# First batch of a sliding-window attention and mixer kernel: last 64 tokens as a group of their own, scores in halves, two pairs loaded raw

## The chip, the cores and the metric

The kernel runs on one core of one Trainium2 chip. Its engines are TensorE (PE; its weight loads are shown as PEld), VectorE (DVE), ScalarE (ACT), GpSimd (POOL) and SyncE (SP), each with an instruction stream of its own that runs in order; SP, ScalarE and POOL also issue DMA transfers. The metric is the time of one execution on the device in microseconds (us). Each kernel is run several times, and the median counts.

## The reference

Eight batches of causal attention over a window of 128 tokens with a linear bias per head, and a mixer over tokens and channels behind it:

```python
scores = q @ k.T / sqrt(64) - slope[h] * |i - j|        # 8 batches, 8 heads, 576 tokens, 64 wide
mask   = (i - j >= 0) & (i - j < 128)
x      = softmax(where(mask, scores, -1e9)) @ v         # heads side by side: (8, 576, 512)
u      = x + (relu(x.T @ w_tok1) @ w_tok2).T            # over tokens: 576 -> 256 -> 576
out    = u + relu(u @ w_ch1) @ w_ch2                    # over channels: 512 -> 1536 -> 512
```

Inputs and output are float32 in memory; matmuls run on bf16.

## The kernel before

Tokens are cut into blocks of 128: four blocks and a tail of 64 per batch. Scores are held transposed (keys on partitions), so that the exponential's result is at once the left operand of the product with v; v carries a column of ones, whose product is the softmax's sum. A block needs the keys of its own block and of the one before ("kind" 1 and 0). Each exponential is multiplied on VectorE with a table `masks` (or `maskt` for tails) that holds exp(-slope x distance) and zeros; for two head pairs of the first batch the bias is instead added by TensorE into the score's bank before the exponential (`BIAS`, matmuls of `slant` by `dist`, line 948).

Nothing is scheduled by hand. Every step is a `plan.op` with an engine, a cost in ns, a rank and the buffers that it makes, uses or reads; `Plan.run` plays the program through once while it is built, with the written costs and a model of the load queue, always starting the step that can begin first and then the one of least rank. The order in which steps were started becomes the order of each engine's instructions. Where the plan sees TensorE wait over 250 ns within the first 60 us, it puts in matmuls of zeros (line 1513). Constants such as `WIDE`, `START` or `WARM` are numbers of that plan; they give no instruction.

PSUM has eight banks of 512 columns. Scores take pairs of banks: `TWO` is (0,1) and (2,3). Single results take one of `ONE`, banks 4 to 7; some take `ANY`.

The program has these parts: `opening` (batch 0's attention and token mixing, head pair by head pair), then for every batch b `main` (hidden layer `uT` by `WC1`, line 1280, and output layer by `WC2` and its sums `WT`, line 1457) together with `side` (attention and token mixing of batch b+1, scores line 711, values line 769, mixing lines 814 to 892).

In `opening` a head pair hp goes through
- `turn`: 8 transposes each of q and k (line 926), copied out of PSUM to `qkT` (line 929),
- `score`: into all four banks 0 to 3, two per head of the pair: the bias (line 948), 14 score matmuls of the four blocks and four of the tail (line 968), two exponentials of 1024 columns (line 975), for pairs 2 and 3 the multiplication (line 985). The tail's scores stand in the place that block 0 would have for a block before it; so the first score needs the tail's q and k,
- `value`: products with v for each head (line 1011), reciprocal and norm (lines 1019, 1022), then the tail's own (lines 1046 to 1053),
- `mix`: both token matmuls, the residual, and the transposes for the hidden layer (lines 1066 to 1118). The first hidden-layer matmuls are those at line 1266.

Pair hp's `value` and `mix` are created right after `score` of pair hp+1.

At the start SP and ScalarE load q and k of pair 0 and of the tail as float32 (`raws`, lines 485 and 487), and VectorE casts them (lines 560, 563). All other loads are issued by POOL in the order of `LOADS`, cast to bf16 on the way, at most eight under way: q and k of pairs 1 to 3 (line 544), v (line 537), the blocks of batch 1 (line 528; q4 to q7, tails last) and the weights (line 549; W: token layers, A: quarters of `WC1`, B: quarters of `WC2`). A load into a buffer that is still read waits on POOL, and all later ones behind it. From batch 2 on q and k are transposed by DMAs on SP's queue (line 663), among the stores of the output.

Of the kernel before, what the change touches and what calls it, by code (L numbers as in the profile page):

```python
# [20 lines left out]
class Buf:  # L21
    def __init__(self, ring, choice):
        self.ring, self.choice, self.slot = ring, choice, None
        self.writers, self.parts, self.users, self.later = [], {}, [], []

# [5 lines left out]
class Ring:  # L31
# [23 lines left out]
    def take(self, b):  # L55
        b.slot = self.best(b.choice)[1]
        for i in b.slot:
            self.owner[i] = b
            self.log[i].append(b)
# [6 lines left out]
class Plan:  # L66
# [60 lines left out]
    def run(self):  # L127
# [25 lines left out]
        free = {"PE": 1500.0, "ACT": 5600.0, "DVE": 3300.0, "POOL": 1250.0, "SP": 1300.0}  # L153
# [57 lines left out]
        while todo:  # L211
            best = None
            for e, c in cand.items():
                pick, early = None, None
                for o in c:
# [9 lines left out]
                    for b in o.bufs:  # L225
                        if b.slot is None:
                            got = b.ring.best(b.choice, asked.count(b.choice))
                            asked.append(b.choice)
# [77 lines left out]
    def emit(self, spin):  # L306
# [12 lines left out]
        for _, _, go in sorted(work, key=lambda w: w[:2]):  # L319
# [6 lines left out]
PIECES = 3  # L326
HOLD = 2
# [4 lines left out]
WIDE = 1000  # L332
# [16 lines left out]
SECOND_LATE = False  # L349
BANKS = 8  # L350
# [3 lines left out]
START = 2400.0  # L354
# [14 lines left out]
FIRST_BLOCK = (2, 3)  # L369
# [3 lines left out]
def kernel(  # L373
# [48 lines left out]
    ANY = ONE + [(0,), (1,), (2,), (3,)]  # L422

# [20 lines left out]
    raws = [const.tile([P, DM], F32, name=f"raw{i}") for i in range(3)]  # L444
    plan.ring("ob", raws + [sb.tile([P, DM], F32, name=f"ob{i}") for i in range(3)])
# [38 lines left out]
    for raw, t, eng in ((raws[0], q, nc.sync), (raws[1], k, nc.scalar)):  # L484
        eng.dma_start(out=raw.rearrange("p (h n) -> p h n", h=2), in_=wide_rows(t, 0))
    for i, (t, eng) in enumerate(((q, nc.sync), (k, nc.scalar))):
        eng.dma_start(out=raws[2][i * R : (i + 1) * R, :].rearrange("p (h d) -> p h d", h=H), in_=rows(t, 0, NC * P, R))
# [16 lines left out]
    for e in range(2):  # L504
        for i, h in enumerate(HEADS[e]):
            act_.activation(out=masks[:, e, i, :, :], in_=dist[:, 0:2, :], func=ACT.Exp, scale=-float(slopes[h]))
# [50 lines left out]
    for i_, name in enumerate("qk"):  # L557
        raw = raws[i_]
        buf = block(0, 0)["qk"]
        block(0, 0)[name] = plan.op("DVE", 455, lambda raw=raw, buf=buf, i="qk".index(name): dve_.tensor_copy(  # L560
            out=buf()[:, i, :, :], in_=raw.rearrange("p (h d) -> p h d", h=H)), -1e6, makes=buf, after=4.4e3 + 600 * i_)
    for i in range(2):
        plan.op("DVE", 455, lambda i=i, buf=last["qk"]: dve_.tensor_copy(
            out=buf()[0:R, i, :, :], in_=raws[2][i * R : (i + 1) * R, :].rearrange("p (h d) -> p h d", h=H)), -1e6 + 1,
            makes=last["qk"], after=5.4e3 + 500 * i)
    lo_ = {}
    for h in [h for h in range(2, H) if h // 2 in BIAS + FIRST_BLOCK]:
# [6 lines left out]
    lw1, lw2, lw2t, lc1, lc2, later = [], [], [], [], [], []  # L574
    for item in LOADS.split():
# [7 lines left out]
        elif what == "W":  # L583
            if n == 1:
                lw1 += weights([(W1[:, 0:NC, :], w1, 512, 2080)] +
                               [(W1p[i * R : (i + 1) * R, i, :], moe_w_tok1[NC * P : S, :], 64, 420) for i in range(2)])
            else:
                lw2 += weights([(W2[:, :, :], w2[:, :, 0 : NC * P], 256, 2630)])
        elif what == "T":
            lw2t += weights([(W2t[:, :, :], w2[:, :, NC * P : S], 256, 300)])  # L590
        elif what == "A":
            hs = slice(n * DCH // 4, (n + 1) * DCH // 4)
            lc1 += weights([(WC1[:, :, hs], c1[:, :, hs], 512, 2500)]) * (NHT // 4)
# [43 lines left out]
    for e in range(2):  # L637
# [5 lines left out]
        mt.append(plan.op("DVE", 1300, go, 0, after=30e3))  # L643
# [47 lines left out]
    def scores(pr, blk, half, rank, behind=()):  # L691
# [32 lines left out]
        for e in range(2):  # L724
# [9 lines left out]
            def mask(es=es):  # L734
# [4 lines left out]
                         needs=mt if tail and half != 0 else [])  # L739
# [58 lines left out]
    def token_mix(b, rank):  # L798
# [20 lines left out]
        def tails():  # L819
            for j in range(NJ):  # L820
# [8 lines left out]
                uses=[xt] if xt else [], needs=lw1, mode=0 if pad else 1)  # L829
# [76 lines left out]
    def opening(rank):  # L906
# [7 lines left out]
        def turn(hp):  # L914
# [632 lines left out]
```

## Time and profile before

| | us |
|---|---|
| median of 3 runs | 283.03 |
| lowest and highest run | 281.44, 283.85 |
| the profiled execution: span | 281.4 |
| its TensorE busy | 271.3 |
| its VectorE busy | 209.9 |
| its ScalarE busy | 136.1 |
| its POOL busy | 115.7 |

The profiled execution's time is its span, from the first instruction to the last; it stands at the lower end of the runs. Times of single rows are counted from the span's start. A timeline row reads: start, length, engine, line, operation, output <- inputs, shape, how many; in brackets how long the engine had been idle before it and what it then waited for. A row on a load ends with the time from its issue to its landing. TensorE is busy nearly throughout, so a saving on another engine counts only where TensorE waits for it.

### The profile page before, as it was taken

How to read it: one execution, taken by the hardware profiler on the slowest of the kernel's cores; microseconds unless marked ns; L12 is line 12 of the kernel's file. 1: busy time of each engine (PE TensorE's matmuls, PEld its weight loads, DVE VectorE, ACT ScalarE, POOL GpSimd, SP SyncE). 2: the span in 40 equal slices, each digit the busy share in tenths (PEclk: the TensorE clock that was granted, in tenths of full speed). 3: DMA queues.
4: the chain of work that ended last, by engine and by line, in shares of the span. 5: the costliest groups of instructions: out<-in, count | busy, mean ns of one | idle time of the engine just before them, and what ended most of it. 6: DMA issues, size and time to landing. Idle time of an engine off the chain costs nothing.

```text
span 281.4 us, 7149 instructions
## 1 busy us (share of the span) xinstructions
PE 271.3 (96%) x2890; PEld 183.2 (65%) x2890; DVE 209.9 (75%) x493; ACT 136.1 (48%) x215; POOL 115.7 (41%) x148
## 2 busy tenths in 40 slices
PE   5799999999999999999999999999999999999994
PEld 3577556577577745486657745486657755489983
DVE  6359778998798749683979459683979469697972
ACT  6365778132983268305962069206962078205500
POOL 8998596840089105900386006900480320012000
PEclk9799999999999999999999999999999999999999
DMA  8999999999999996999799997999799830042014
GB/s 157 161 132 178 180 155 186 154 145 170 186 73 127 176 227 57 142 144 181 169 123 151 187 223 51 143 150 196 140 128 117 203 98 2 19 112 115 2 51 137
DMA packets 160337, 38.32 MB, mean 136 GB/s; under 512 B 146544, under 2 KB 159472, under 8 KB 160304
## 3 DMA queue, kind: packets, MB, share of 16 engines
q0 software_dynamic: 110512, 19.90, 90.0%
q1 hardware_dynamic: 48992, 17.57, 34.1%
q8 instruction: 22, 0.36, 0.6%
q10 hardware_dynamic: 800, 0.39, 0.5%
q14 instruction: 11, 0.09, 0.1%
HBM read 35.85 MB, written 9.44 MB: 161 GB/s over the span
## 4 chain that ended last, share of the span: by engine, by line
PE 87%; DVE 6%; DMA 3%; ACT 2%; issue 1%; SPq 0%; DVEq 0%; ACTq 0%
PE ps L1457 25%; PE ps L1280 24%; PE ps L769 5%; PE ps L711 5%; PE ps L857 4%; PE ps L1323 4%; PE ps L814 4%; PE ps L1368 4%; PE ps L1204 3%; DMA raw<-in_q_dram 3%; DVE WT L612 1%; PE ps L1266 1%; PE ps L968 1%; PE ps L892 1%; PE ps L853 1%; PE ps L1011 1%
## 5 line engine op out<-in xcount | busy, mean ns | idle before, releaser
L1286 ACT ACTIVATE r<-ps 128x512 bf16<-128x512 f32 x74 | 43.6, 602 | 78.9 <-PE ps L1280 73.0
L1280 PE MATMUL ps<-uT,WC 128*128 128x512 bf16 x324 | 79.4, 379 | 0.0
L528 POOL DMA_DIRECT2D v<-in_v_dram x36 | 30.5, 849 | 90.9 <-PE ps L769 87.6
L726 ACT ACTIVATE pe<-ps 128x1024 bf16<-128x1024 f32 (+1 forms) x64 | 55.3, 916 | 3.0 <-PE ps L711 2.3
L1280 PEld LDWEIGHTS <-WC 128*128 128x128 bf16 x324 | 28.5, 98 | 28.5 <-issue 0.7
L1457 PEld LDWEIGHTS <-r 128*128 128x128 bf16 x384 | 37.0, 98 | 8.5 <-issue 1.8
L736 DVE TENSOR_TENSOR pe<-pe,mask 128x1024 bf16<-128x1024 bf16 (+1 forms) x56 | 34.1, 619 | 10.2 <-ACT pe L726 9.7
L528 POOL DMA_DIRECT2D qk<-in_q_dram x35 | 30.4, 871 | 4.7 <-DMA WC<-in_moe_w_ch_dram 2.4
L528 POOL DMA_DIRECT2D qk<-in_k_dram x35 | 30.4, 872 | 3.7 <-DMA WC<-in_moe_w_ch_dram 1.9
L1457 PEld LDWEIGHTS <-s 128*128 128x128 bf16 x288 | 28.1, 98 | 4.7 <-DVE s L1305 0.2
L1457 PE MATMUL ps<-WC,r 128*128 128x256 bf16 x192 | 25.4, 273 | 0.0
L785 DVE TENSOR_TENSOR xb<-ps,rt 128x256 bf16<-128x256 f32 (+1 forms) x61 | 24.8, 418 | 0.6
L1457 PE MATMUL ps<-WT,s 128*128 128x256 bf16 x192 | 23.7, 273 | 0.1
L1457 PE MATMUL ps<-WT,r 128*128 128x256 bf16 x192 | 23.7, 273 | 0.0
L769 PEld LDWEIGHTS <-pe 128*128 128x128 bf16 (+1 forms) x480 | 18.3, 99 | 7.7 <-DVE pe L736 2.1
L769 PE MATMUL ps<-v,pe 128*128 128x65 bf16 (+1 forms) x480 | 22.1, 194 | 0.1
L875 DVE TENSOR_TENSOR ub<-ps,xb 128x512 bf16<-128x512 f32 x32 | 19.8, 682 | 2.0 <-PE ps L857 2.0
L711 PEld LDWEIGHTS <-qkT 64*128 64x128 bf16 x480 | 12.9, 94 | 9.3 <-issue 7.2
L1440 POOL DMA_DIRECT2D out_dram<-ob x5 | 3.6, 718 | 35.6 <-DVE ob L1428 35.4
L782 DVE RECIPROCAL rt<-ps 128x4 f32<-128x4 f32 (+1 forms) x64 | 10.4, 176 | 8.8 <-PE ps L769 8.5
L711 PE MATMUL ps<-qkT 64*128 64x128 bf16 (+1 forms) x256 | 16.8, 218 | 0.0
L1428 DVE TENSOR_TENSOR raw<-ps,ub 128x512 f32<-128x512 f32 x16 | 10.7, 686 | 6.3 <-PE ps L1457 6.3
(131 smaller groups left out, 396.9 us busy)
## 6 DMA issues: line engine op xcount, KB each, us to landing
qk<-in_q_dram POOLq DMA_DIRECT2D x31, 128.0 KB, 5.8
qk<-in_k_dram POOLq DMA_DIRECT2D x31, 128.0 KB, 6.0
v<-in_v_dram POOLq DMA_DIRECT2D x28, 128.0 KB, 6.2
out_dram<-raw SPq DMA_DIRECT2D x13, 256.0 KB, 4.3
WC<-in_moe_w_ch_dram POOLq DMA_DIRECT2D x8, 384.0 KB, 8.2
out_dram<-ob SPq DMA_DIRECT2D x11, 256.0 KB, 2.7
out_dram<-ob POOLq DMA_DIRECT2D x5, 256.0 KB, 2.9
v<-in_v_dram POOLq DMA_DIRECT2D x16, 64.0 KB, 3.9
```

The lines of the kernel that those rows point to most:

```text
L528: nc.gpsimd.dma_start(out=to()[p0 : p0 + n, :, :], in_=rows(src, b, s0, n))
L711: pe_.matmul(wide(e)[:, i, kind, a:z], lhsT=ts[kb]()[e * D : (e + 1) * D, NHP + i, :], rhs=ts[blk]()[e * D : (e + 1) * D, i, a:z], start=T ...
L726: act_.activation(out=pb()[:, e, :, lo:, c0:c1_], in_=wide(e)[:, :, lo:, c0:c1_], func=ACT.Exp, scale=scale)
L736: dve_.tensor_tensor(out=o, in0=o, in1=heads(mk, es), op=ALU.mult)
L769: pe_.matmul(view()[a:z, at, i, :], lhsT=pb()[:, e, i, kind, a:z], rhs=vb()[:, h, 0 : D + 1], start=m == 0, stop=m == len(mms) - 1, skip_g ...
L785: dve_.tensor_tensor(out=x4(), in0=view()[r0:r1_, :, :, 0:D], in1=rt()[r0:r1_, 0:n, :, :].broadcast_to([r1_ - r0, n, 4, D]), op=ALU.mult)
L814: pe_.matmul(t1[j]()[:, :], lhsT=W1[:, c, j * P : (j + 1) * P], rhs=xb()[:, blk, :], start=c == 0, stop=False)
L857: pe_.matmul(ht()[:, hs], lhsT=W2[:, j, c * P : (c + 1) * P], rhs=r1()[:, j, :], start=j == 0, stop=j == NJ - 1 and not fold)
L875: plan.op("DVE", 690, lambda blk=blk, ht=ht, hs=hs: dve_.tensor_tensor(out=ub()[:, blk, :], in0=ht()[:, hs], in1=xb()[:, blk, :], op=ALU.a ...
L1280: pe_.matmul(ct()[:, :], lhsT=WC1[:, cb, t * P : (t + 1) * P], rhs=uT()[:, cb, :], start=cb == 0, stop=cb == NCB - 1)
L1286: plan.op("ACT", 600, lambda t=t, ct=ct: act_.activation(out=r2()[:, t, :], in_=ct()[:, :], func=ACT.Relu), rk, part=(r2, t), uses=[ct], o ...
L1457: pe_.matmul(bk()[:, c * HN : (c + 1) * HN], lhsT=l(t, c), rhs=w(t), start=first, stop=g == 1 and t == HK - 1, skip_group_check=True)
```

## The change

In `opening`:
- The tail leaves `score` and `value` and becomes `ends`: one bank pair with the scores of all eight heads' 64 last tokens, one exponential, one multiplication, one set of value products, one reciprocal and one norm. It is created after pair 2's `value`.
- `score` makes two halves of two blocks. A half holds both heads in one pair of banks, taken from (0,1), (2,3) and (4,5). The first half's exponential has 768 columns, since block 0 has no block before it; the second's has 1024. Pairs 2 and 3 are multiplied in three steps: 512, 256 and 1024 columns. Their bias matmuls for block 0 go.
- q and k of pair 1 too are loaded raw by SP and ScalarE, ahead of the tail's, and cast on VectorE or ScalarE.
- Ranks are written out: scores and transposes by pair, values 1.5 pairs later, `ends` after 2.5, all of `mix` after 3 or more.
- `masks` is made by steps that the plan orders.

`LOADS` begins with v0, q2, k2; W1 comes after q3 and k3; `WC1`'s quarters come in the order 0, 2, 1, 3; one of the two copies of the last token rows (`W1p`) moves behind batch 1's blocks. A buffer may have a gate: `second`'s and `unit`'s banks are then taken from banks 4 to 7 alone until the next batch's last score has been started in the plan. Costs and due times of the plan change.

```diff
+    def options(self):
+        if self.gate and self.gate[0] is not None and self.gate[0].t0 is None:
+            return self.gate[1]
+        return self.choice
...
-LOADS = ("q1 k1 v0 v8 q2 k2 v1 W1 q3 k3 v2 v3 W2 q4 k4 v4 A0 q5 k5 v5 "
-         "A1 A2 A3 q6 k6 v6 q7 k7 v7 T0 lq8 lk8 lv8 B0 B1 B2 B3")
+LOADS = ("v0 q2 k2 v1 q3 k3 v8 W1 v2 v3 W2 A0 q4 k4 A2 v4 A1 q5 k5 v5 A3 "
+         "q6 k6 v6 q7 k7 v7 P0 T0 lq8 lk8 lv8 B0 B1 B2 B3")
...
-FIRST_BLOCK = (2, 3)
...
+    SPS = TWO + TWICE[:MORE]
...
-    raws = [const.tile([P, DM], F32, name=f"raw{i}") for i in range(3)]
-    plan.ring("ob", raws + [sb.tile([P, DM], F32, name=f"ob{i}") for i in range(3)])
+    raws = [const.tile([P, DM], F32, name=f"raw{i}") for i in range(2 * RAW + 1)]
+    plan.ring("ob", raws + [sb.tile([P, DM], F32, name=f"ob{i}") for i in range(5 - 2 * RAW)])
...
-    for raw, t, eng in ((raws[0], q, nc.sync), (raws[1], k, nc.scalar)):
-        eng.dma_start(out=raw.rearrange("p (h n) -> p h n", h=2), in_=wide_rows(t, 0))
+    for hp in range(RAW):
+        for raw, t, eng in ((raws[2 * hp], q, nc.sync), (raws[2 * hp + 1], k, nc.scalar)):
+            eng.dma_start(out=raw.rearrange("p (h n) -> p h n", h=2), in_=wide_rows(t, hp))
...
-                               [(W1p[i * R : (i + 1) * R, i, :], moe_w_tok1[NC * P : S, :], 64, 420) for i in range(2)])
+                               [(W1p[0:R, 0, :], moe_w_tok1[NC * P : S, :], 64, 250)])
...
+        elif what == "P":
+            lw1p += weights([(W1p[R:P, 1, :], moe_w_tok1[NC * P : S, :], 64, 250)])
...
         def score(hp):
-            sp = [bank(TWO) for _ in range(2)]
...
+            for part in range(2):
+                sp = bank(SPS)
+                blks = [2 * part, 2 * part + 1]
...
+                def go(blks=blks, wide=wide):
+                    f = t().rearrange("p a b -> p (a b)")
+                    for i, blk in enumerate(blks):
+                        own = slice(blk * P, (blk + 1) * P)
+                        for kind in (1, 0) if blk else (1,):
+                            kb = blk - 1 + kind
+                            for e in range(2):
+                                es = slice(e * D, (e + 1) * D)
+                                pe_.matmul(wide(e)[:, i, kind, :], lhsT=f[es, KO + kb * P : KO + (kb + 1) * P], rhs=f[es, own],
+                                           stop=True, start=hp not in BIAS, skip_group_check=True)
...
+                x = plan.op("ACT", 172 + 2 * (DM - a) / 1.2, expo, rk, uses=[sp], part=(pb, ("x", part)),
+                            **({} if part else {"makes": pb}))
...
+        def ends():
+            rk = -1e6 + ENDS_AT
+            tt = qkT[0, TAIL]
+            sp, pb = bank(SPS), plan.buf("pe")
...
+            plan.op("PE", 260, go, rk, makes=sp, uses=[tt] + ts, reads=[(x, 1) for x in ts], mode=1)
...
+            plan.op("ACT", 1026, lambda: act_.activation(out=flat(), in_=sp()[:, :], func=ACT.Exp, scale=scale), rk,
+                    makes=pb, uses=[sp])
+            plan.op("DVE", 700, lambda: dve_.tensor_tensor(
+                out=p4(), in0=p4(), in1=masks[:, :, :, :, 0:R].rearrange("p e i k c -> p (e i) k c"), op=ALU.mult), rk,
+                adds=pb, needs=mk_ops[0] + mk_ops[1])
...
+            plan.op("PE", 480, value, rk, makes=ots, uses=[pb, vt] + [held[0, hp]["v"] for hp in range(NHP)], mode=2)
...
         for hp in range(NHP):
             turn(hp)
             score(hp)
             if hp:
                 value(hp - 1)
-                mix(hp - 1)
+        ends()
         value(NHP - 1)
-        mix(NHP - 1)
+        for hp in range(NHP):
+            mix(hp)
```

More of the change, by code (lines that the diff above doesn't have):

```diff
@@ L738, in scores @@
             op = plan.op("DVE", 154 + len(es) * n / 1.92, mask, rank, part=(pb, e), reads=[(pb, ("x", i)) for i in es],
-                         needs=mt if tail and half != 0 else [])
+                         needs=mk_ops[e] + (mt if tail and half != 0 else []))
             if one:
@@ L972, in score @@
[L972 to L978 removed]
+            done = []
@@ L998, in value, with rest @@
+                def rest():
+                    o = pb()[:, :, 0, 1, :]
+                    dve_.tensor_tensor(out=o, in0=o, in1=masks[:, :, hp, 1, :], op=ALU.mult)
+                done[-1] = plan.op("DVE", 154 + (1 + part) * 267, most, rk, needs=mk_ops[0] + mk_ops[1] + [x], part=(pb, ("m", part)))
+                if not part:
+                    done.append(plan.op("DVE", 287, rest, rk, needs=mk_ops[0] + mk_ops[1] + [x], part=(pb, "r")))
+            pb.parts[0] = pb.parts[1] = done
         def value(hp):
+            rk = -1e6 + VALUE_AT + hp * STEP
@@ L1508 @@
                 o.behind.append(marks["score"])
+            for x in gates:
+                x[0] = marks["score"]
         base += n
```

202 lines of the change are left out of this document (106 added, 96 removed).

## The prediction

> **What bounds the kernel now.** I read the page first, then the busy times by stage, the timeline of the first 60 us engine by engine, the landings of single loads, and last the instruction orders of both programs.
>
> ```profile
> span 281.4 us, 7149 instructions
> PE 271.3 (96%) x2890; PEld 183.2 (65%) x2890; DVE 209.9 (75%) x493; ACT 136.1 (48%) x215; POOL 115.7 (41%) x148
> PE   5799999999999999999999999999999999999994
> PE 87%; DVE 6%; DMA 3%; ACT 2%; issue 1%; SPq 0%; DVEq 0%; ACTq 0%
> ```
>
> TensorE carries 87% of the chain that ended last; only the first slices and the last one have room. By stage (edges at the first exponential, the end of the last one, and the two ends of the mixing of batch 1; the columns after the length are busy us of PE, PEld, DVE, ACT, POOL, then granted clock, DMA share, GB/s):
>
> ```profile
> 0.00:12.70 12.70, 7.99 (x82) 5.21 (x84) 6.39 (x28) 6.08 (x13) 11.40 (x21) 0.87 1.18 157
> 12.70:24.60 11.90, 11.25 (x209) 8.82 (x210) 8.13 (x25) 8.69 (x11) 11.90 (x15) 1.00 1.69 148
> ...
> 44.80:58.80 14.00, 13.58 (x143) 8.38 (x141) 13.66 (x33) 5.34 (x12) 8.77 (x10) 1.00 2.08 161
> 58.80:277.30 218.50, 218.49 (x2219) 148.26 (x2218) 165.58 (x364) 101.20 (x155) 69.08 (x85) 1.00 1.16 130
> ```
>
> From 58.8 to 277.3 us TensorE is busy 218.49 of 218.5 us: nothing can be won there. From the second hidden layer of batch 0 on, TensorE's instruction order is the same in both programs. So the question is only how many us earlier TensorE reaches that common part. The room is in the first 25 us; 44.8 to 58.8 is a second narrow place, where VectorE is busy 13.66 of 14 us.
>
> What holds the first stage shows in the timeline (start, length, engine, line):
>
> ```profile
> 4.72 1.04 DVE L560 CAST qk<-raw 128x512 bf16<-128x512 f32 x2
> 7.16 0.41 PE L926 MATMUL ps<-ident,qk 128*64 128x128 bf16 x8 [0.84 <-DMA qk<-in_q_dram]
> 8.43 1.02 DVE L563 CAST qk<-raw 64x512 bf16<-64x512 f32 x2 [2.67 <-DMA raw<-in_q_dram]
> 8.91 0.44 PE L674 MATMUL ps<-ident,qk 128*128 128x128 bf16 x4 [1.34 <-DVE qk L563]
> 11.69 0.29 PE L968 MATMUL ps<-qkT 64*128 64x128 bf16 x2
> 12.73 1.94 ACT L975 ACTIVATE pe<-ps 128x1024 bf16<-128x1024 f32 x2 [1.42 <-PE ps L968]
> 13.81 0.60 PE L948 MATMUL ps<-dist,slant 128*128 128x256 bf16 x4
> 15.25 0.23 PE L968 MATMUL ps<-qkT 64*128 64x128 bf16 x2
> 15.91 1.94 ACT L975 ACTIVATE pe<-ps 128x1024 bf16<-128x1024 f32 x2 [1.24 <-PE ps L968]
> 19.19 1.94 ACT L975 ACTIVATE pe<-ps 128x1024 bf16<-128x1024 f32 x2 [0.71 <-PE ps L968]
> 22.59 1.94 ACT L975 ACTIVATE pe<-ps 128x1024 bf16<-128x1024 f32 x2 [0.98 <-PE ps L968]
> 23.83 0.55 DVE L985 TENSOR_TENSOR pe<-pe,mask 128x768 bf16<-128x768 bf16 x1
> 27.12 0.61 PE L674 MATMUL ps<-ident,qk 128*128 128x128 bf16 x8
> 28.84 0.39 PE L1266 MATMUL ps<-uT,WC 128*128 128x512 bf16 x1
> ```
>
> Two things. The first score waits for the 64 tail tokens, whose raw q lands at 8.43 and which then need cast, transpose and copy: score 11.69, exponential 12.73. After that the four head pairs come every 3.2 to 3.4 us although their exponentials take 1.94: a pair fills all four of the score banks 0 to 3, so the next pair's matmuls (bias 13.81 and on, scores 15.25) begin only as its exponentials have read them.
>
> **The change, part by part.** *Score halves and three bank pairs.* A half now needs two banks of six, so ScalarE can run its exponentials one behind the other. Four halves have 1024 columns (0.97 each, from 1.94 for two), four have 768, between this row's 0.600 for 512 and 0.97: I take 0.78.
>
> ```profile
> L726 ACT ACTIVATE pe<-ps 128x512 bf16<-128x512 f32 x2 | 1.2, 600 | 0.3 <-PE ps L711 0.3
> 6.14 1.07 ACT L929 COPY qkT<-ps 128x512 bf16<-128x512 bf16 x2 [0.28 <-PE ps L926]
> 3.31 2.56 ACT L506 ACTIVATE mask<-dist 128x256 bf16<-128x256 bf16 x8
> 1.29 0.70 ACTq L487 DMA_DIRECT2D raw<-in_k_dram  x1
> ```
>
> *The tail as its own group* takes it out of the first score's path; it adds one exponential (0.97) and moves the tail's value product behind three pairs. Its matmuls are as many as before (16 score, 16 value, narrow). On VectorE four small reciprocal and norm pairs give way to one mask, one reciprocal and one norm of 64 partitions by 512, about equal. *The start.* ScalarE has one more load to issue (0.70), so its table load and masks end later: seven masks (7 x 0.32 = 2.24) from about 4.0 to 6.25, then the two copies (1.07) to 7.35. TensorE transposes q of pair 1 before the first scores, so that raw load must have landed. It now stands on SP's queue where the tail's q stood:
>
> ```profile
> 0.74 0.44 SPq L485 DMA_DIRECT2D raw<-in_q_dram x1
> raw<-in_q_dram SPq DMA_DIRECT2D x1, 256.0 KB, 3.6
> raw<-in_q_dram SPq DMA_DIRECT2D x1, 128.0 KB, 7.2
> raw<-in_k_dram ACTq DMA_DIRECT2D x1, 128.0 KB, 5.1
> ```
>
> Bounds for its landing: 4.3 (0.74 + 3.6, the load ahead of it) and 8.45 (the tail's q in that place). I take 6.4, the landing of the tail's k (1.29 + 5.1), since it too is one of two second loads. Cast 0.52, eight transposes 0.41: 7.35. First exponential at about 8.0 (0.66 lay between first score and exponential at full clock, 15.25 to 15.91), with bounds 7.4, which the copies set, and 10.
>
> From there ScalarE has 4 x 0.97 + 4 x 0.78 + 0.97 (tail) + two copies 1.07 = 9.05 us of work, so its last exponential can end at 17.1. The other limit is the load of pair 3's k:
>
> ```profile
> 11.01 0.76 POOL L544 DMA_DIRECT2D qk<-in_k_dram x1
> qk<-in_k_dram POOLq DMA_DIRECT2D x1, 128.0 KB, 3.8
> 8.49 0.74 POOL L549 DMA_DIRECT2D W<-in_moe_w_tok_dram  x1 [0.35 <-DMA qk<-in_k_dram]
> 9.22 1.09 POOL L549 DMA_DIRECT2D W1p<-in_moe_w_tok_dram  x2
> ```
>
> It lands at 14.8 now. Two q/k loads leave POOL's queue, and v8, W1 and both W1p go behind it: six issues less in front (0.74 + 1.09 for three of them, about 0.75 each for the rest, 4.1 us), so it is issued near 6.9 and lands between 10.7 (3.8 after issue) and 14.8. I take the middle, 12.7. From it to the last exponential: transposes 0.4, copy 0.6, the tail's scores, mixing and two halves of scores on TensorE about 1.7, exponentials of tail and pair 3 about 2.7: 18.1. With gaps I take **18.4**, bounds 17.1 and 20.5; before it is 22.59 + 1.94 = 24.53.
>
> *Order behind it.*
>
> ```profile
> 33.57 0.69 DVE L736 TENSOR_TENSOR pe<-pe,mask 128x1024 bf16<-128x1024 bf16 x1
> 47.19 0.42 DVE L736 TENSOR_TENSOR pe<-pe,maskt 128x512 bf16<-128x512 bf16 x1
> ```
>
> The mixes of all pairs now come after all scores, so between the last exponential and the first hidden-layer matmul (before 24.53 to 28.84, 4.3 us) VectorE has more to do: a masked pair has three multiplies (1024 columns 0.69, 512 columns 0.42, 256 columns estimated at 0.29) where two of 0.55 stood, and the tail's norm is queued among them. I take 5.5, bounds 4.3 and 7. The first hidden-layer matmul then comes at 23.9, 4.9 us earlier. The old order had by then done one transposition more (0.61): **4.3 us** of head start.
>
> *Loads.* W1, W2 and the first quarter of the hidden weights keep about their times; the quarters come in the order of use. The second W1p is wanted only by batch 1's mix. The load of v4 overwrites pair 0's v and so waits on POOL until the tail's values have been multiplied (tail's exponential at 18.4 less two of pair 3, 16.7, and its mask 0.69: 17.4), and A1 and all later loads queue behind it; four loads issued before it cover that wait. Four bias matmuls of 256 columns go (0.60 for four) and four become half as wide; they lie inside the first stage, where ScalarE sets the pace, and I count nothing for them. The two added casts (0.52 each) fall where VectorE waited 2.67 us. Gates, due times and cost constants emit no instruction: cost nothing, since TensorE's order behind batch 0 is unchanged. SP's later transposes and stores keep their kinds and nearly their order; the load for batch 2's fourth block stands behind one store more, which is ready 4 us earlier.
>
> *The second narrow place.* Batch 0's output products need all of the last weights:
>
> ```profile
> 39.14 0.75 POOL L549 DMA_DIRECT2D WC<-in_moe_w_ch_dram  x1 [0.16 <-DMA W2t<-in_moe_w_tok_dram]
> WC<-in_moe_w_ch_dram POOLq DMA_DIRECT2D x1, 384.0 KB, 9.2
> 51.02 0.82 PE L1457 MATMUL ps<-WC,r 128*128 128x256 bf16 x6
> 52.23 1.48 PE L1457 MATMUL ps<-WC,r 128*128 128x256 bf16 x12
> ```
>
> The last quarter lands at 48.3; the products that need it start at 52.23. So only 3.9 us of head start can pass, less 0.4 for some four matmuls of such products that only the old order has run by then (0.82 for six), unless the train of loads itself runs earlier. Two loads of it have moved to other queues, worth 0 to 1.6 us (two issues of about 0.8). I take 0.5 us: 47.8, and a gain of 4.0, of which I give back 0.3 for the longer stall between the last block's scores and values, where no hidden-layer chunk is left to fill it. **Sum: 4.3 us won in the first stage, 3.7 us at the common part and at the end.** 281.4 - 3.7 = 277.7 for the profiled execution; the median of the runs, 283.03, stands 1.6 above that span, so **279.3**.
>
> The Trainium skill (DMA: Bandwidth & Descriptors, section Issuing engines are not separate DMA queues) speaks against the raw loads: loads from SP, ScalarE and GpSimd run on the same 16 DMA engines, so that another issuing queue saves only issue time. The trace agrees: the tail's q, 128 KB, took 7.2 us beside POOL's loads where 256 KB ahead of it took 3.6. By that rule the train does not run earlier, which is rival one.
>
> **The rivals.** *One: the loads take it back.* Pair 1's q and k travel as f32, 256 KB each instead of 128; 256 KB more at the first stage's 157 GB/s is 1.6 us on every later load. For it: a DMA share above 1 in every stage quoted. Against it: the same bytes are read from memory, and POOL drops two loads. The last weights land at 49.9, the gain is 52.23 - 49.9 - 0.4 = 1.9: 281.1. Chance 0.18.
>
> *Two: the first stage gains little,* because pair 3's k lands at 14.8 as now and VectorE's queue stretches the rest to 7 us: 20.5 + 7 = 27.5, less 0.6: a gain of 0.7, 282.3. For it: VectorE is busy 8.13 of 11.9 us even now. Against it: W1 and W1p do leave the front of that queue. Chance 0.06.
>
> *Three: the clock ends it slower.* In the first 12.7 us the granted clock was 0.87, that is 1.65 us lost, after TensorE had stood idle for 1.34 us before 8.91. The new start has short pieces with waits between them; if TensorE runs at half clock from about 8 us, its 11 us or so of opening work (11.25 busy in the second stage) take 22 and the hidden layer starts near 8 + 22 + 2 of waits = 32, 3.2 us later than 28.84: 286.2. It is slower than before from about 5 us of lost clock on. Against it: 1.00 from 12.7 us on in a stage that waits as often. The Trainium skill (TensorE: Matmul & The Clock Gate, Part 1) gives the rule: half clock after an idle window of about 3.4 us until as long a busy one; here no wait of the trace is that long, and the loss of 1.65 us fits one such window. Chance 0.08.
>
> **How the numbers follow.** The forecast has 0.68. A run of this kernel differs from another by up to 0.9% (281.44 to 283.85), so 1%, 2.8 us, is what I count as a change. Its own bounds: best, train 1.6 us earlier, 5.1 us won, 277.9; worst, about 2.8. The range goes one us below the best for the spread of runs and up to rival two: 276.9 to 282.3. Faster takes the forecast, 0.68; same takes rivals one and two, 0.24, less 0.02 for a further loss on top of rival two; slower takes that and rival three, 0.10.
>
> **What would show it.** First exponential near 8 us, not 12.7; ScalarE's nine exponentials nearly without gaps, the last ending near 18.4; first hidden-layer matmul near 24; first products on the last weights near 48; 1.00 busy from there with the old spacing. Wrong if pair 1's raw q lands after 8 us, if the last weights land near 50, if the clock stays at 0.5 past 13 us, or if the order behind batch 0 opens gaps on TensorE.

## The result, and the profile after

| | before | after |
|---|---|---|
| median of 6 runs each, same chip, us | 283.21 | 279.44 |
| lowest and highest run | 280.94, 283.85 | 278.79, 279.68 |
| span of the profiled execution | 281.4 | 277.6 |

The ratio is 0.9883, with a 95% interval of 0.9847 to 0.9918: faster by 1.2%, clear of the noise of the runs. Run again beside the later experiments, on another chip, the changed kernel had a median of 279.33 us and a ratio of 0.9897 (0.986 to 0.9935). Forecast were 279.3 us, and 277.7 for the profiled execution.

The page of the changed kernel (span; busy time and instructions of each engine; busy tenths of TensorE and its granted clock in 40 slices; the engines' shares of the chain that ended last):

```profile
span 277.6 us, 7099 instructions
PE 266.5 (96%) x2848; PEld 182.0 (66%) x2881; DVE 209.7 (76%) x489; ACT 138.4 (50%) x219; POOL 114.7 (41%) x146
PE   5989999999999999999999999999999999999994
PEclk9999999999999999999999999999999999999998
PE 86%; DVE 8%; ACT 4%; issue 1%; ACTq 0%
```

The page of the kernel before has this row for the clock:

```profile
PEclk9799999999999999999999999999999999999999
```

The 7 in its second slice is a piece of the result that I had not put down as one; the section on the hardware comes back to it. The opening by stages after the change (columns as in the prediction; edges at the first exponential, the end of the last one and the first hidden-layer matmul):

```profile
0.00:8.00 8.00, 5.08 (x61) 4.00 (x63) 5.58 (x27) 5.28 (x13) 7.07 (x14) 1.00 0.99 199
8.00:17.80 9.80, 8.94 (x194) 7.09 (x193) 8.31 (x22) 8.95 (x13) 8.63 (x12) 1.00 1.67 178
17.80:23.40 5.60, 5.13 (x75) 4.11 (x76) 4.64 (x13) 2.81 (x9) 5.55 (x7) 1.00 1.82 177
```

In the second stage ScalarE is busy 8.95 of 9.80 us, where it had been busy 8.69 of 11.90: it now sets the pace of the scores, as the change wants. The timeline of the changed kernel shows the points that the prediction named, pair 1's cast, the exponentials with ScalarE's one wait among them, and the first hidden-layer matmul, then POOL's issues of pair 3's k and of the last two quarters of `WC2`:

```profile
4.78 1.84 DVE L584 CAST qk<-raw 128x512 bf16<-128x512 f32 x4
...
8.00 3.52 ACT L1006 ACTIVATE pe<-ps 128x768 bf16<-128x768 f32 x4
...
12.87 0.59 ACT L960 COPY qkT<-ps 128x512 bf16<-128x512 bf16 x1 [0.64 <-PE ps L957]
13.35 1.73 ACT L1006 ACTIVATE pe<-ps 128x768 bf16<-128x768 f32 x2
14.98 1.02 ACT L1086 ACTIVATE pe<-ps 128x1024 bf16<-128x1024 f32 x1
16.04 1.73 ACT L1006 ACTIVATE pe<-ps 128x1024 bf16<-128x1024 f32 x2
...
23.43 0.38 PE L1327 MATMUL ps<-uT,WC 128*128 128x512 bf16 x1
...
6.75 0.71 POOL L567 DMA_DIRECT2D qk<-in_k_dram  x1
...
36.55 1.52 POOL L572 DMA_DIRECT2D WC<-in_moe_w_ch_dram  x2 [0.25 <-DMA v<-in_v_dram]
```

The view of its loads has for pair 3's k and for the last quarter, from issue to landing:

```profile
qk<-in_k_dram POOLq DMA_DIRECT2D x1, 128.0 KB, 4.7
...
WC<-in_moe_w_ch_dram POOLq DMA_DIRECT2D x1, 384.0 KB, 9.5
```

The last exponential ends at 17.77 (before 24.53), the hidden layer starts at 23.43 (before 28.84), and the last weights land at 46.8 (36.55, half of 1.52 for the issue ahead, 9.5) where they had landed at 48.3. So 5.4 us are won by 23.4, and 3.8 are left at the end. The experiments ask which parts of the change carry the first number, and what takes the difference.

### The profile page after: what moved, and what is told of

It reads as the page before. It is cut to its first block, busy times and chain, and to the rows that moved or that the text cites. A ratio compares the mean times of both kernels' runs of the same rounds, so it can differ in the third digit from the quotient of the medians.

```text
span 277.6 us, 7099 instructions
## 1 busy us (share of the span) xinstructions
PE 266.5 (96%) x2848; PEld 182.0 (66%) x2881; DVE 209.7 (76%) x489; ACT 138.4 (50%) x219; POOL 114.7 (41%) x146
## 4 chain that ended last, share of the span: by engine, by line
PE 86%; DVE 8%; ACT 4%; issue 1%; ACTq 0%
PE ps L1519 25%; PE ps L1341 24%; PE ps L741 5%; PE ps L799 5%; PE ps L1384 4%; PE ps L844 4%; PE ps L887 4%; PE ps L1429 4%; PE ps L1265 3%; DVE WT L642 1%; ACT r L1347 1%; ACT pe L756 1%; DVE ub L905 1%; PE ps L982 1%; DVE pe L766 1%
## 5 line engine op out<-in xcount | busy, mean ns | idle before, releaser
L1341 PE MATMUL ps<-uT,WC 128*128 128x512 bf16 x304 | 77.2, 380 | 1.0
L1490 DVE TENSOR_TENSOR raw<-ps,ub 128x512 f32<-128x512 f32 x27 | 18.3, 684 | 10.4 <-PE ps L1519 10.3
L799 PEld LDWEIGHTS <-pe 128*128 128x128 bf16 (+1 forms) x480 | 18.4, 99 | 7.5 <-DVE pe L766 2.1
L1502 POOL DMA_DIRECT2D out_dram<-raw x6 | 4.3, 717 | 34.1 <-DVE raw L1490 34.1
L1490 DVE TENSOR_TENSOR raw<-ps,raw 128x512 f32<-128x512 f32 x19 | 12.9, 688 | 7.1 <-PE ps L1519 7.0
```

Source lines behind the costliest of these rows:

```text
L799: pe_.matmul(view()[a:z, at, i, :], lhsT=pb()[:, e, i, kind, a:z], rhs=vb()[:, h, 0 : D + 1], start=m == 0, stop=m == len(mms) - 1, skip_g ...
L1341: pe_.matmul(ct()[:, :], lhsT=WC1[:, cb, t * P : (t + 1) * P], rhs=uT()[:, cb, :], start=cb == 0, stop=cb == NCB - 1)
L1490: dve_.tensor_tensor(out=v, in0=bk().rearrange("p (c n) -> p c n", c=2), in1=src, op=ALU.add)
```

## The experiments

### Each part undone alone

Five kernels undo one part each; the plan then orders everything anew. The first four shared a chip and runs of the kernel before (median 282.37), the fifth ran beside the changed kernel itself.

All scores wait for the tail again:

```diff
+            late = list(qkT[0, TAIL].writers)
...
-                marks["first"] = plan.op("PE", (4 - (not part)) * 57, go, rk, uses=[t], reads=[(t, 0), (t, 1)], mode=1,
+                marks["first"] = plan.op("PE", (4 - (not part)) * 57, go, rk, uses=[t], reads=[(t, 0), (t, 1)], needs=late, mode=1,
```

> Every score of the first batch waits again for the transposed tail; the tail keeps its own group. Theory (the chain of exponentials in the opening sets the head start, and a shift of it passes on to the end): first exponential at 10 to 11 us instead of 8.0, last one ending 1.5 to 2.5 us later than 17.8, first hidden-layer matmul as much later than 23.4, and the end 1.0 to 2.5 us later. Rival (what counts lies behind the opening: the train of loads or VectorE between 40 and 57 us): the opening moves as above, but the end by less than 0.5 us.

A pair's scores wait until the pair before has had all its exponentials:

```diff
+            late = list(marks.get("exps", []))
+            marks["exps"] = []
...
-                    plan.op("PE", 440 - 110 * (not part), bias, rk, makes=sp, needs=[lo_[2 * hp + e] for e in range(2)] if hp else [])
+                    plan.op("PE", 440 - 110 * (not part), bias, rk, makes=sp, needs=late + ([lo_[2 * hp + e] for e in range(2)] if hp else []))
...
-                marks["first"] = plan.op("PE", (4 - (not part)) * 57, go, rk, uses=[t], reads=[(t, 0), (t, 1)], mode=1,
+                marks["first"] = plan.op("PE", (4 - (not part)) * 57, go, rk, uses=[t], reads=[(t, 0), (t, 1)], needs=late, mode=1,
...
+                marks["exps"].append(x)
```

> A pair's bias and score matmuls wait for both exponentials of the pair before it, as when a pair filled all score banks; halves, tail group and loads stay. Theory: pairs start 2.8 to 3.0 us apart instead of about 1.8 to 2.7, the last exponential ends 1 to 2 us after 17.8, the end comes 0.5 to 1.5 us later. Rival (pair 3's load is what the last exponential waits for, so the banks do not matter): last exponential and end within 0.3 us.

Pair 1 is loaded by POOL again, in the place that it had:

```diff
-RAW = 2
+RAW = 1
...
-LOADS = ("v0 q2 k2 v1 q3 k3 v8 W1 v2 v3 W2 A0 q4 k4 A2 v4 A1 q5 k5 v5 A3 "
+LOADS = ("q1 k1 v0 q2 k2 v1 q3 k3 v8 W1 v2 v3 W2 A0 q4 k4 A2 v4 A1 q5 k5 v5 A3 "
```

> q and k of pair 1 go back to POOL's queue, first in its order. Theory: pair 1's k lands at 8 us instead of 6, pair 3's 1.3 us later, last exponential 0.5 to 1.3 us later, end 0.3 to 1.2 us later. Rival (raw loads move f32 on the same 16 engines and delay all others): later loads land up to 1.6 us sooner and the end comes 0 to 0.5 us earlier.

The order of loads is the old one, less pair 1:

```diff
-LOADS = ("v0 q2 k2 v1 q3 k3 v8 W1 v2 v3 W2 A0 q4 k4 A2 v4 A1 q5 k5 v5 A3 "
-         "q6 k6 v6 q7 k7 v7 P0 T0 lq8 lk8 lv8 B0 B1 B2 B3")
+LOADS = ("v0 v8 q2 k2 v1 W1 P0 q3 k3 v2 v3 W2 q4 k4 v4 A0 q5 k5 v5 "
+         "A1 A2 A3 q6 k6 v6 q7 k7 v7 T0 lq8 lk8 lv8 B0 B1 B2 B3")
```

> The load list of the kernel before, without q and k of pair 1: v8, W1 and both halves of W1p ahead of pair 3, quarters of WC1 after the blocks of batch 1 as they were. Theory: pair 3's k lands near 13.5 instead of 11.5 us, the last exponential ends 1 to 2 us later, the end comes 0.7 to 1.7 us later. Rival (ScalarE's queue and not the load sets the last exponential): last exponential and end within 0.4 us.

Score halves have two pairs of banks in place of three:

```diff
-MORE = 1
+MORE = 0
```

> The first batch's scores get two pairs of banks again in place of three; all else as in the changed kernel. Theory that each part is worth its own delay of the last exponential: that exponential ends 0.3 to 1.0 us later and the end follows by as much. Theory that any delay there is multiplied (tail's values late, v4's load and all behind it on GpSimd's queue late, VectorE's order planned anew): end 1.5 to 3.5 us later than the changed kernel.

And the changed kernel beside it:

> The changed kernel itself, so that it shares a chip and the runs of the kernel before with the three that follow. Both theories: ratio 0.985 to 0.992, profiled span 277.0 to 278.2, last exponential of the first batch ends 17.5 to 18.1, first hidden-layer matmul at 23.2 to 23.8, last quarter of the second hidden layer's weights lands 46.5 to 47.3.

| | last exponential ends | first hidden-layer matmul | median | ratio to before, interval |
|---|---|---|---|---|
| changed kernel again | 17.98 | 23.66 | 279.33 | 0.9897 [0.986, 0.9935] |
| scores wait for the tail | 20.35 | 28.15 | 283.43 | 1.0034 [1.0003, 1.0066] |
| a pair at a time | 19.81 | 26.07 | 281.19 | 0.9965 [0.9937, 0.9993] |
| pair 1 by POOL | 20.42 | 28.14 | 282.9 | 1.0022 [0.9987, 1.0056] |
| old order of loads | 18.90 | 26.25 | 282.67 | 1.0012 [0.9983, 1.004] |
| two pairs of banks | 19.19 | 25.46 | 281.3 | 0.9976 [0.9946, 1.0006] |

The first two columns are from the profiled execution. That of "pair 1 by POOL" is the slowest of its twelve runs (284.78), so its two times may be late ones.

Every part is needed: the losses of the five, 1.9 to 4.1 us in the medians, or 0.7 to 1.4% by the ratios, which compare within a chip, add up to several times the gain of the whole, so they are not shares of it. The delay of the last exponential (0.9 to 2.4 us) explains the time of the second one only (1.83 us there, 1.86 in the median, where its theory had 0.5 to 1.5). The fifth lost 1.97 us for a delay of 1.21, within the range of the theory that a delay is multiplied when the plan orders anew; the first, third and fourth, whose hidden layer starts 2.6 to 4.5 us later, lost 3.3 to 4.1, more than their expectations had.

For the old order of loads the trace shows what else is late. In the timeline stand POOL's issues of v4 and of the first quarter of `WC1`, and the hidden layer's first matmul:

```profile
18.93 0.88 POOL L551 DMA_DIRECT2D v<-in_v_dram  x1 [3.15 <-PE ps L1100]
19.79 0.77 POOL L572 DMA_DIRECT2D WC<-in_moe_w_ch_dram  x1
...
26.25 0.59 PE L1327 MATMUL ps<-uT,WC 128*128 128x512 bf16 x2
```

The view of loads gives that quarter's landing:

```profile
WC<-in_moe_w_ch_dram POOLq DMA_DIRECT2D x1, 384.0 KB, 6.2
```

There v4 stands ahead of the first quarter; its issue waits 3.15 us until the tail's values are done, and the quarter behind it waits with it. The quarter lands at 26.0 and the hidden layer begins 0.25 later. In the changed kernel that quarter is issued at 13.3. For the first, third and fifth I take the new order to be the rest of the loss; no run takes it apart further. Nine of the first one's twelve runs also show a mean granted clock of 0.988 to 0.994.

The gates need no run: with `GATE = False` the program that is built is the same, instruction for instruction.

### A later landing of the last weights

One load of 384 KB more goes ahead of the last four quarters. All engines keep their order.

```diff
+    extra = WS[:, 0, :, :].rearrange("p a n -> p (a n)").rearrange("p (j c) -> p j c", j=3)
...
+            if n == 0:
+                def both(own=lc2[-1].emit, js=js):
+                    nc.gpsimd.dma_start(out=extra, in_=c2[:, js, :])
+                    own()
+                lc2[-1].emit = both
```

> One further load of 384 KB is issued ahead of the last four quarter loads of weights, into a buffer not yet in use then; every engine's order stays the same. At 157 GB/s it takes 2.4 us, so that the last quarter lands at about 49.3 in place of 46.9. Theory of the landing (the prediction's step 4: the head start passes only up to that landing): end 1.5 to 1.9 us later than the changed kernel, ratio to it 1.005 to 1.007. Theory of VectorE (the stretch from 40 to 57 is set by VectorE's own work, the weights are there in time): 0 to 0.5 us later.

Measured: 279.84 us, ratio 0.9923 (0.9895 to 0.9951), 0.5 above the changed kernel. From this kernel's timeline, the hidden layers of batch 0 and of batch 1 begin, and POOL issues the last three quarters:

```profile
23.14 0.38 PE L1333 MATMUL ps<-uT,WC 128*128 128x512 bf16 x1
...
59.12 1.89 PE L1347 MATMUL ps<-uT,WC 128*128 128x512 bf16 x8
...
36.04 2.27 POOL L573 DMA_DIRECT2D WC<-in_moe_w_ch_dram  x3 [0.20 <-issue]
```

From its view of loads, the last quarter from issue to landing:

```profile
WC<-in_moe_w_ch_dram POOLq DMA_DIRECT2D x1, 384.0 KB, 10.7
```

From its view of waits between 76 and 82 us, TensorE's longest (in total, times, longest):

```profile
PEld L747 <- DMA qkT<-qk: 1.6, 1, 1.6
```

The changed kernel beside it, which has no such wait, by the timeline:

```profile
23.66 0.38 PE L1327 MATMUL ps<-uT,WC 128*128 128x512 bf16 x1
...
59.64 1.67 PE L1341 MATMUL ps<-uT,WC 128*128 128x512 bf16 x7
...
36.91 1.51 POOL L572 DMA_DIRECT2D WC<-in_moe_w_ch_dram  x2 [0.31 <-DMA v<-in_v_dram]
```

And its last quarter:

```profile
WC<-in_moe_w_ch_dram POOLq DMA_DIRECT2D x1, 384.0 KB, 8.9
```

The last quarter lands at 48.2 (two thirds of 2.27 after 36.04, plus 10.7) instead of 46.6, and from one hidden layer to the next it is 35.98 us in both. So the landing of the last weights does not hold the stretch, not even 1.6 us later. What holds comes at 78 us: batch 2's scores wait 1.6 us for their q and k, which SP's queue transposes. This kernel also came there half a microsecond earlier, for its whole opening was by that much earlier than the other's; so the two causes of that wait are not parted here. The kernel without fills, below, has no added load, came 0.4 us early too, and waits 0.9 us at the same place; the one without weight sums came 1.0 early and waits 0.6. So an earlier arrival is not passed on in full: these transposes are the next limit, and no run takes it away.

### A later opening, without a new plan

ScalarE makes three more exponentials ahead of the tail's, and every order stays.

```diff
+    spare = WS[:, 0, 0, 0 : 2 * P].rearrange("p (a n) -> p a n", a=2)
...
+    tail = [o for o in plan.ops if o.eng == "ACT" and o.cost == 1026][0]
+    def more(own=tail.emit):
+        for _ in range(3):
+            act_.activation(out=spare, in_=dist[:, 0:2, :], func=ACT.Exp, scale=-1.0)
+        own()
+    tail.emit = more
```

> ScalarE makes three further exponentials of 256 columns (1.0 to 1.2 us) ahead of the tail's exponential; every engine's order is otherwise the changed kernel's. The last exponential then ends at 18.9 to 19.2. Prediction's steps 3 and 4 (the head start passes on one for one up to its limit, and is over 1 us above that limit at the first hidden-layer matmul): first hidden-layer matmul 1.0 to 1.2 us later, end 0 to 0.6 us later. Theory that the end follows the last exponential one for one: 0.9 to 1.3 us later. Theory that a delay is multiplied even without a new plan: over 1.5 us later.

From the timeline of this kernel, ScalarE's added work, the tail's exponential and the last pair's; then the two hidden layers' beginnings:

```profile
14.96 1.32 ACT L1584 ACTIVATE WS<-dist 128x256 bf16<-128x256 bf16 x3
16.19 1.01 ACT L1087 ACTIVATE pe<-ps 128x1024 bf16<-128x1024 f32 x1
17.09 1.72 ACT L1007 ACTIVATE pe<-ps 128x1024 bf16<-128x1024 f32 x2
...
24.47 0.38 PE L1328 MATMUL ps<-uT,WC 128*128 128x512 bf16 x1
...
60.39 0.81 PE L1342 MATMUL ps<-uT,WC 128*128 128x512 bf16 x3
```

The window in which its TensorE waits for the added work:

```profile
16.40:19.80 3.40, 1.91 (x38) 1.50 (x36) 2.51 (x8) 3.23 (x7) 1.17 (x3) 1.00 1.73 180
```

The last exponential ends at 18.81, 0.83 later than in the changed kernel beside it; the hidden layer starts 0.81 later, that of batch 1 0.75 later, and the span is 278.5, 1.0 longer. One for one, then, for a delay with the orders kept, and no limit on the way that would have taken up a part: this is the second theory's number. The limit that the prediction saw further on (steps 3 and 4 in the text above) would have left 0 to 0.6. The median went up more, to 281.44 (ratio 0.9972, 0.994 to 1.0004): six of the twelve runs have a mean granted clock of 0.988 to 0.993 and a median of 281.64, the other six 280.53, 1.2 above the changed kernel.

### What fills the stretch from 40 to 57 us

The fills that TensorE makes between 41 and 44 us are left out:

```diff
-            if a < FILL and z - a > 250:
+            if a < FILL and z - a > 250 and not 40e3 < a < 44e3:
```

> The 16 matmuls on zeros with which TensorE fills its waits between 41 and 44 are left out; nothing else changes. If they only fill waits for the attention of batch 1 (VectorE's mask at 41.9, ScalarE's copy that ends at 43.6): 0 to 0.2 us earlier, TensorE idle for 1.5 us in their place, and the granted clock stays at 1.00. If they are longer than the waits: 0.3 to 1.0 us earlier.

VectorE's eight sums of second-layer weights are left out, and their products take a column half of the weights themselves:

```diff
-                    dve_.tensor_tensor(out=WT[:, i, a, :], in0=x, in1=y, op=ALU.subtract)
+                    pass
...
-            return lambda t: WT[:, i, t, :]
+            return lambda t: WC2[:, t + HK * (i > 0), HN:DM]
```

> VectorE's eight sums of second-layer weights (0.45 to 0.57 us each, between 43.9 and 52.3) are left out, and the products that use them take a column half of the weights themselves, so that this part of the result is not computed; TensorE's order and work stay. Theory that VectorE sets the stretch from 40 to 57 throughout: end 0.8 to 2.0 us earlier than the changed kernel. Theory that what was lost there is lost before 44, where batch 1's exponentials, masks and values follow one another with no other matmul ready: 0 to 0.4 us earlier, TensorE's lost time from 40 to 50 still 1.7 us or more.

Two of batch 1's residuals go from VectorE to TensorE and ScalarE:

```diff
+FOLD1 = (4, 6)
...
-            fold = wide and blk % 2 == 1
+            fold = wide and blk % 2 == 1 or b == 1 and blk in FOLD1
```

> The residual of two of batch 1's blocks is added by TensorE into the bank and copied out by ScalarE, in place of two additions on VectorE. Theory of VectorE: two additions of about 0.6 us go from its chain between 40 and 57, TensorE gets some 0.4 us more work: end 0.5 to 1.2 us earlier than the changed kernel. Theory of the landing: nothing gained there, TensorE's added work stays: 0 to 0.4 us later.

| | from one hidden layer's start to the next | span | median | ratio to before, interval |
|---|---|---|---|---|
| changed kernel again | 35.98 (23.66 to 59.64) | 277.5 | 279.33 | 0.9897 [0.986, 0.9935] |
| without the fills | 36.02 (23.20 to 59.22) | 277.8 | 279.97 | 0.9932 [0.9904, 0.9959] |
| without the weight sums | 35.07 (23.53 to 58.60) | 276.9 | 278.27 | 0.9877 [0.9848, 0.9905] |
| residuals moved | 36.28 (23.45 to 59.73) | 278.9 | 281.12 | 0.9968 [0.9943, 0.9992] |

The changed kernel's TensorE and VectorE at 41 us, from its timeline:

```profile
41.61 1.20 PE L1577 MATMUL ps<-zero 128*128 128x512 bf16 x10
42.67 0.42 PE L799 MATMUL ps<-v,pe 128*128 128x65 bf16 x8
42.93 0.66 PE L1577 MATMUL ps<-zero 128*128 128x512 bf16 x6
...
41.93 0.68 DVE L766 TENSOR_TENSOR pe<-pe,mask 128x1024 bf16<-128x1024 bf16 x1
```

The kernel before had these fills in place of them, and six more ahead of batch 1's hidden layer:

```profile
45.64 0.33 PE L1513 MATMUL ps<-zero 128*128 128x128 bf16 x3
...
46.65 0.33 PE L1513 MATMUL ps<-zero 128*128 128x128 bf16 x3
...
48.84 0.34 PE L1513 MATMUL ps<-zero 128*128 128x128 bf16 x3
...
58.34 0.50 PE L1513 MATMUL ps<-zero 128*128 128x128 bf16 x6
```

Batch 0's hidden layer now ends at 40, and batch 1's last pairs go through exponential, mask and value products with nothing beside them: values start at 42.67, as the mask that begins at 41.93 is done. 1.86 us of fills (1.20 + 0.66) stand where 1.00 stood, or 1.50 with the six at 58.34. They do not cause the loss: without them the stretch is as long (36.02), the granted clock stays at 1.00, and the kernel is no faster; they stand in waits. It came to 59 us 0.4 earlier than the changed kernel, as it had started, and lost that in this wait (view of waits, 76 to 82 us):

```profile
PEld L741 <- DMA qkT<-qk: 0.9, 1, 0.9
```

Without the weight sums (the busy times by window of that kernel, then of the changed one, columns as in the prediction) VectorE has 2.45 us less to do from 40 to 50, and TensorE is full from 50 on:

```profile
40.00:50.00 10.00, 9.91 (x141) 6.99 (x141) 6.97 (x21) 5.51 (x12) 7.06 (x9) 1.00 1.84 178
50.00:60.00 10.00, 10.00 (x87) 7.22 (x86) 9.39 (x17) 2.54 (x5) 5.64 (x8) 1.00 2.16 139
```

```profile
40.00:50.00 10.00, 9.92 (x138) 6.87 (x138) 9.42 (x25) 5.59 (x11) 7.46 (x10) 1.00 1.72 177
50.00:60.00 10.00, 9.78 (x84) 6.94 (x83) 9.52 (x19) 2.26 (x4) 6.14 (x8) 1.00 2.02 153
```

The stretch is 0.91 us shorter and the median 1.06 lower (the span 0.6). So VectorE does set a part of it: eight sums, 4.4 us by their rows, cost 0.9. That is the first theory's range; of the second, the fills before 44 stand there all the same, but its 0 to 0.4 us was too small. Moving residuals was a miss for both. It made the stretch no shorter (36.28), and the new plan that came with it lost more behind: from 90 to 105 us its TensorE is busy 14.40 us where the changed kernel's is busy 15.00.

### The wait of v4

The issue of v4 goes behind q5 and k5; the other engines keep their order.

```diff
+    begun = {}
...
+        begun[item] = plan.orders
...
+    loads = {o.order: o for o in plan.ops if o.eng == "POOL"}
+    loads[begun["v4"] + 1].t0 = loads[begun["k5"] + 1].t0 + 1
```

> v4's load is issued after q5 and k5 instead of ahead of them; every other engine keeps the changed kernel's order. GpSimd's queue then no longer stands from 16.8 to 18.1 for the tail's values, and A1, q5, k5 and what follows are issued about 1.2 us earlier. Prediction's step 5 (the loads issued ahead of it cover that wait): end within 0.3 us of the changed kernel. Rival (that wait sets the loads, and these the end): 0.5 to 1.2 us earlier.

Measured: 279.96 us, ratio 0.9917 (0.9888 to 0.9946). It tells less than it should have, for POOL then waits as long ahead of q4:

```profile
16.06 0.89 POOL L551 DMA_DIRECT2D qk<-in_q_dram  x1 [1.28 <-DVE pe L1020]
```

In the changed kernel the wait was 1.31 us, ahead of v4 at 18.07. A1 came out at about 18.5 instead of 18.94, not 1.2 us earlier. The wait moved and nothing was won: batch 1's hidden layer begins at 60.76, 1.1 us later than in the changed kernel. What those loads would be worth without any wait stays open.

## Why the prediction was right

The number was right within 0.2 us, and the first stage mostly for the reasons given. The second narrow place was not; that its size came out is luck.

**The start (step: first exponential at about 8.0).** It came at 8.00. Pair 1's raw q was put between 4.3 and 8.45 and at 6.4; its cast is part of a group of four that ends at 6.62 (4.78 + 1.84), so it landed by then.

**ScalarE's chain (18.4, bounds 17.1 and 20.5).** 17.77. A pair's two halves, one of 768 and one of 1024 columns, were put at 0.78 + 0.97 and took 1.73. Of the two limits the prediction took the later one, pair 3's k, for 18.4; that k landed at 11.45 (6.75 + 4.7) and not at 12.7, since W1 and v8 really had left the queue ahead of it. What ended last was the other limit, ScalarE's own work, put at 17.1: it ran with one wait of 0.64 us for transposes, at 12.87, and with no gap from 13.35 on. The later opening showed that a delay in this chain passes on one for one.

**From the last exponential to the hidden layer (5.5, bounds 4.3 and 7).** 5.66; rival two, which had 7 after an exponential at 20.5, fell with it. The head start at that point is 5.4 us, less 0.61 for the transposition 4.8, where 4.3 was forecast.

**The second narrow place.** Here the argument failed, and its size held. The prediction let the head start through only up to the landing of the last weights (4.0) and then gave back 0.3 "for the longer stall between the last block's scores and values, where no hidden-layer chunk is left to fill it". The landing does not hold: 1.6 us later it changed nothing there, and a later opening was not taken up by it. The row that I read as a wait for weights, 52.23, was an instruction that stood in its order behind VectorE's work (a matmul at 51.93 takes the copy that VectorE begins at 51.58); no view said that it waited for a load.

A premise failed with it. The prediction had TensorE's order the same in both programs "from the second hidden layer of batch 0 on". In the programs as built the orders agree, but for buffer numbers, only from just ahead of these rows on (before, then changed):

```profile
68.13 1.06 PE L1323 MATMUL ps<-uTt,WC 128*128 128x128 bf16 x16
```

```profile
64.47 1.06 PE L1384 MATMUL ps<-uTt,WC 128*128 128x128 bf16 x16
```

Ahead of them batch 1's attention and batch 0's output products are put in a new order. So 4.8 us of head start went in, 3.7 came out at these rows and 3.8 at the end. The prediction let 4.0 of its 4.3 through and priced the stall at 0.3. The 1.0 that was given back is more than that. A longer stall is part of it: the fills for batch 1's last pairs take 0.86 us more than the three groups in their place, and all fills on the way 0.69 more (2.19 us, with 0.33 at 28.23, for 1.50). Whether that is most of the 1.0 stays open, since no run has the new opening with the old order behind it. That 4.0 - 0.3 and 4.8 - 1.0 meet within 0.1 is luck.

**The loads.** Rival one had the train 1.6 us later; it ran 1.5 us earlier (46.8 for 48.3), as the upper bound of the forecast said. By the Trainium skill (DMA: Bandwidth & Descriptors, Issuing engines are not separate DMA queues) another issuing queue saves only issue time. The trace agrees in size: two issues of about 0.75 us went from POOL. The prediction read the rule as no gain at all, which was rival one; the issue time that the rule leaves is the size that came. POOL's waits for buffers differ in the two programs as well, so that these issues are the whole 1.5 is not shown.

**v4 and the gates.** The gates cost nothing, which the orders show. That four loads cover v4's wait is neither shown nor refuted.

**The clock.** Rival three did not come: the granted clock is 1.00 in every stage quoted. But the other half of its argument had been on the table and I did not use it: 1.65 us of the time before had been lost to the clock. The part of the gain that comes from this is the next section's subject. The prediction's 12.73, 24.53 and 28.84 all contain it, so its sum of the first stage was right for the profiled execution, and too large for a run before that kept its clock. In these results a run's time is about 1.9 us above its own span. So the profiled execution before, with 281.4, did not stand at the lower end of the runs but took about 283.3; that the median stood "1.6 above that span" came out nearly right because the median, 283.03, is by its time a run that had lost its clock too.

## What to carry to other kernels

Before pricing a stage from a profile, look at the granted clock within it and at how many runs have that clock; a gain may partly be a clock that is no longer lost. A resource that is ready shortly before its use is not yet a wall: check what the user was waiting for, and test it by delaying the resource alone with the order kept. Where two programs are taken to do the same from some point on, find that point in both before a head start is carried through it. Where parts of a change are undone one by one under a planner, the losses don't add up, and an added delay with a fixed order gives the cleaner price.

## What the runs showed of the hardware

The kernel before loses its clock in the opening in some of its runs and not in others. Its profiled execution is one that did; by windows, columns as before with the granted clock third from the end:

```profile
6.00:9.30 3.30, 1.12 (x24) 0.63 (x18) 0.84 (x2) 1.66 (x3) 2.95 (x5) 0.97 1.85 173
9.30:12.60 3.30, 3.14 (x37) 2.11 (x36) 0.85 (x2) 0.59 (x1) 3.30 (x6) 0.51 1.42 146
```

The same windows of the changed kernel:

```profile
6.00:9.30 3.30, 2.37 (x46) 1.78 (x42) 1.48 (x4) 3.13 (x7) 3.29 (x6) 1.00 1.72 188
9.30:12.60 3.30, 3.30 (x77) 2.68 (x77) 2.87 (x9) 2.75 (x4) 3.30 (x5) 1.00 1.63 187
```

Where TensorE was busy 1.12 of 3.30 us, half clock followed for 3.3 us; where it was busy 2.37, none did. Of the 97 runs of the kernel before beside the experiments, 38 have a mean granted clock of 0.986 to 0.994, with medians of 282.96 to 283.04 on the three occasions; the other 59, at 0.996 or more, have medians of 281.06 to 281.18. Eight of these 59 took 283.6 to 284.0 us all the same, and nothing here shows why. All twelve runs of the changed kernel are at 0.997 or more; of 48 runs of four kernels that share its opening (more load, no fills, no weight sums, residuals moved), one is below 0.996, at 0.991. So about half of the 3.8 us between the two profiled executions is this clock, and against a run before that kept it the change is worth some 1.7 us (279.33 for 281.06). No run changed the clock alone, so the halves are read from the runs' clocks and not tested apart.

The Trainium skill (TensorE: Matmul & The Clock Gate, Part 1) has half clock after an idle window of about 3.4 us, in windows that run freely, whatever the kernel's start. The length agrees, and free windows would explain that the same program loses its clock in 38 of 97 runs. "Idle" is not what the trace shows: if the window is the one just ahead, a third busy was enough. The later opening points the same way: its TensorE is busy 1.91 us in 16.40 to 19.80, where that of the changed kernel is busy 2.71, and six of its twelve runs lost clock; where in those runs, no trace shows.
